# Linear attention and a gated feed-forward in one kernel: batch 0's attention by head halves, another release order of the loads, and a new table of times

## The chip, the cores and the metric

The kernel runs on one core of one Trainium2 chip. The metric is the device time of one execution in microseconds; the time before is the median of three runs. One further execution of each kernel is recorded by the hardware profiler, and all lines of profile shown here come from such records. In them PE is TensorE, DVE VectorE, ACT ScalarE, POOL GpSimd and SP SyncE; L346 is line 346 of the kernel's file.

## What is computed

```python
# q, k, v: (8 batches, 8 heads, 576 tokens, 64) float32;  w_in (512, 2048), w_out (2048, 512) float32
theta = pi/2 * arange(576) / 576
def phi(x):
    r = maximum(x, 0)
    return concatenate([r * cos(theta)[:, None], r * sin(theta)[:, None]], axis=-1)   # 128 features
kv  = einsum('bhsf,bhsd->bhfd', phi(k), v)
z   = sum over the tokens of phi(k)
num = einsum('bhsf,bhfd->bhsd', phi(q), kv)
den = einsum('bhsf,bhf->bhs', phi(q), z)[..., None] + 1e-6
x   = (num / den).transpose(0, 2, 1, 3).reshape(4608, 512)
h   = x @ w_in
out = (h * cos(h)) @ w_out                                                             # (4608, 512) float32
```

## The kernel before

Matrices are held in float16 and accumulated in float32. A batch has 576 tokens: four full tiles of 128 tokens and a remainder of 64. The four full tiles make one chunk of 512 tokens for the feed-forward; the remainders of all eight batches together make a ninth chunk. Chunks 0 to 7 thus follow the batches.

*Attention of one batch.* `load` (L318, L321) brings q, k and v on SP's DMA queue. `prep` (L346 on ACT, L347 on DVE) applies relu and the cosine and sine weights and writes float16 features into the tile `KQ`, one instruction per token tile, and per cosine or sine. `cast_v` (L360 ACT, L361 DVE, L362 POOL) writes v into `V1` beside a column of ones, so that one product gives kv and z. `kv` (L373) runs 40 matmuls (8 heads by 5 token tiles) and copies the result to `kvz`. The q features have to be transposed: for batches 0 and 1 TensorE does it (`q_pe`, L402, with copies to `qT` at L406 and L408); for later batches a DMA transpose on SP's queue does (`q_dma`, L412), which reads `KQ` and writes `qT`. There is one `KQ`, so the next batch's q prep has to wait for those transposes. `num` (L435) multiplies, and three DVE instructions (L451, L453, L455) divide by den; the result is transposed by TensorE (`x_pe`, L475, copy L479) or by a DMA (`x_dma`, L485) into `xT`.

*Feed-forward of one chunk.* `layer1` (L529, chunks 0 and 1; `layer1_plain`, L561, and `layer1_fast`, L667, later) multiplies `xT` by `w_in` into one of four PSUM banks for one group of two 128-column blocks by half of the tokens; `gate` takes the cosine as a Sin on ACT (L502) and multiplies on DVE or POOL (L504). `layer1_fast` and `layer2` (L861) trade matmuls for additions in the manner of Strassen, with copies on ACT (L675, L872) and additions on DVE (L679, L883). `layer2_plain` (L786) is the ordinary second product, used early. Results go through three `ost` buffers to DRAM by DMAs on POOL's queue, some of them accumulating in DRAM.

*What sets the order.* Every piece of work is one step, added to a `Plan` with its reads and writes. Two lists written into the file, `STARTS` (a stamp for each step in hundredths of a microsecond) and `ENGS` (one letter of an engine for each step), fix the engine of each step and the order in which all are issued. The stamps are not waited for on the chip: an engine runs its own steps in the order of their stamps, and waits are semaphores for the data. The 1363 steps of before have stamps from 0 to 275.35 us.

*The head.* `first_attention` (L988) starts with 28 matmuls on unused data (`warm`, L945), loads q whole, k whole and v in two halves of the heads, and takes batch 0 through whole-tile steps; 26 more warm matmuls are spread over the gaps. `weights` (L948) holds the four quarters of `w_in` back by a tiny write on POOL (L950) that reads a piece of k, then issues the four loads on POOL's queue, where they are also turned from float32 to float16 (quarter order 0, 1, 3, 2 by the stamps). A second hold (L960) lets two quarters of `w_out` go after `w_in`'s quarter 0 is there. `second_attention` (L1015) holds batch 1's loads by tiny writes on POOL (`hold_raw`, L975) that read a value of `w_in`'s quarter 2, and `part_of_w_out` (L982) holds the other two quarters of `w_out` until batch 1's q is there (`HOLDW = 1` in the order k, q, v).

```python
def hold():
    nc.gpsimd.tensor_copy(
        out=w_in_sb[0:2, 0, :].rearrange("p (g f) -> p g f", g=4)[:, :, 0],
        in_=raw[ORDER0[1]][0:2, 0, 0, 0:1].broadcast_to((2, 4)))
pl.add("POOL", 0.4, 0.5, 0, hold, hk(ORDER0[1], [0], [0]), [("w_in", g) for g in range(4)])
```

Of the kernel before, what the change touches and what calls it, by code (L numbers as in the profile page):

```python
# [16 lines left out]

STARTS = (
# [166 lines left out]
def kernel(  # L185
# [12 lines left out]
    P = 128  # L198
# [816 lines left out]
    def second_attention():  # L1015
        T = start[1] - 30
        for nm in ORDER1:
# [4 lines left out]
            if nm == ORDER1[HOLDW]:  # L1022
                part_of_w_out(nm, 1)
# [103 lines left out]
```

## Time and profile before

| | before |
|---|---|
| runs, us | 282.57, 281.77, 281.73 |
| median, us | 281.77 |
| profiled execution: span, us | 279.7 |
| PE busy, us | 272.6 (97%), of it warm matmuls 14.7 |
| DVE, ACT, POOL busy, us | 236.9, 210.2, 82.9 |
| mean granted TensorE clock | 1.000 |
| batch 0 landed: q, k, first and second half of v, us | 7.12, 10.43, 12.09, 13.66 |
| `w_in` quarters landed, us | 17.20, 19.72, 22.98, 25.52 |
| `w_out` quarters landed, us | 28.08, 30.79, 44.08, 48.70 |
| batch 1 landed: k, q, v, us | 34.55, 37.86, 40.93 |
| first `layer1` matmul of chunk 1, us | 50.43 |

The span runs from the first to the last instruction of the profiled execution; the time of a run holds some 2 us more. "Landed" is the end of a transfer's last packet, in us from the span's start. A busy PE is one whose matmuls are in flight one behind the other, warm ones included. Releasers behind an arrow name what ended an idle time.

### The profile page before, as it was taken

The numbers are of one execution on the slowest core, as the hardware profiler recorded it, in microseconds if no ns is written. First come the engines' busy times: TensorE is split into PE (matmuls) and PEld (weight loads), VectorE is DVE, ScalarE is ACT, GpSimd is POOL, SyncE is SP. The second block draws the span as 40 slices with busy tenths as digits, with TensorE's granted clock in tenths as the row PEclk, the third lists the DMA queues.
The fourth block names the chain that finished last, engine by engine and source line by source line (L and its number), as shares of the span: only waits on it lengthen the run. The fifth ranks groups of instructions, "written<-read, shape, count | busy, mean of one in ns | idle before, by whom it ended". The sixth has DMA issues, their size and how long they took to land.

```text
span 279.7 us, 6825 instructions
## 1 busy us (share of the span) xinstructions
PE 272.6 (97%) x2698; PEld 215.5 (77%) x2698; DVE 236.9 (85%) x442; ACT 210.2 (75%) x363; POOL 82.9 (30%) x102
## 2 busy tenths in 40 slices
PE   8999999999999999999999999999999999999993
PEld 2567857787966677769777878789988888888882
DVE  1767698989999999999999998989989879873952
ACT  2756699879998897788989988995758686776330
POOL 1430020030501201520340045132534372399210
PEclk9999999999999999999999999999999999999999
DMA  6999989999999999989999998549756495698125
GB/s 207 312 202 206 340 239 241 361 301 174 335 261 271 258 249 246 234 268 259 255 258 246 242 229 284 98 115 141 163 75 139 110 156 105 152 143 123 75 77 150
DMA packets 80223, 58.03 MB, mean 207 GB/s; under 512 B 43200, under 2 KB 77248, under 8 KB 80192
## 3 DMA queue, kind: packets, MB, share of 16 engines
q1 hardware_dynamic: 68960, 39.99, 59.4%
q0 software_dynamic: 10496, 17.04, 30.1%
q10 hardware_dynamic: 736, 0.57, 0.7%
q8 instruction: 21, 0.34, 0.5%
q14 instruction: 10, 0.08, 0.1%
HBM read 36.75 MB, written 11.80 MB: 174 GB/s over the span
## 4 chain that ended last, share of the span: by engine, by line
PE 92%; ACT 3%; DVE 2%; issue 1%; POOL 0%; ACTq 0%; POOLq 0%
PE M L861 34%; PE M L667 14%; PE M L561 11%; PE M L529 9%; PE TR L667 6%; PE ATT L945 5%; PE ATT L435 3%; PE M L786 3%; PE ATT L373 3%; PE TR L561 2%; ACT KQ L346 2%; DVE x L455 1%; PE M L402 1%; PE M L373 0%; PE TR L475 0%
## 5 line engine op out<-in xcount | busy, mean ns | idle before, releaser
L861 PEld LDWEIGHTS <-gT 128*128 128x128 f16 x560 | 53.9, 98 | 8.3
L861 PE MATMUL M<-w_out_sb,gT 128*128 128x256 f16 x448 | 57.1, 273 | 0.0
L504 DVE TENSOR_TENSOR gT<-M,ch 128x512 f16<-128x512 f32 x73 | 48.5, 685 | 5.9 <-ACT ch L502 5.7
L502 ACT ACTIVATE ch<-M 128x512 f32<-128x512 f32 x75 | 43.4, 596 | 12.0 <-PE M L529 5.4
L346 ACT ACTIVATE KQ<-km,CS 128x512 f16<-128x512 f32 x57 | 38.5, 717 | 1.4 <-DMA km<-in_k_dram 1.3
L872 ACT ACTIVATE ost<-M 128x512 f32<-128x512 f32 x41 | 24.3, 596 | 17.9 <-PE M L861 13.0
L346 ACT ACTIVATE KQ<-qm,CS 128x512 f16<-128x512 f32 x46 | 31.5, 720 | 4.1 <-DMA qm<-in_q_dram 4.1
L561 PE MATMUL M<-xT,w_in_sb 128*128 128x512 f16 x136 | 33.8, 379 | 0.0
L861 PE MATMUL M<-T,S 128*128 128x256 f16 x256 | 32.4, 273 | 0.0
L667 PEld LDWEIGHTS <-w_in_sb 128*128 128x128 f16 x288 | 27.3, 98 | 4.8 <-issue 0.3
L362 POOL CAST V<-vm 128x1024 f16<-128x1024 f32 (+1 forms) x18 | 15.9, 907 | 50.8 <-DVE den L451 20.7
L529 PE MATMUL M<-xT,w_in_sb 128*128 128x256 f16 x256 | 30.3, 273 | 0.3 <-DVE gT L504 0.3
L861 PEld LDWEIGHTS <-S 128*128 128x128 f16 x256 | 24.8, 98 | 4.1 <-DVE S L837 0.2
L529 PEld LDWEIGHTS <-w_in_sb 128*128 128x128 f16 x256 | 24.4, 98 | 3.9 <-issue 0.5
L679 DVE TENSOR_TENSOR Z<-M,Z 128x512 f32<-128x512 f32 x31 | 21.1, 687 | 4.3 <-PE M L667 3.1
L561 PEld LDWEIGHTS <-w_in_sb 128*128 128x128 f16 x160 | 14.9, 98 | 12.2
L504 POOL TENSOR_TENSOR gT<-Z,ch 128x512 f16<-128x512 f32 x5 | 6.3, 1268 | 56.6 <-ACT ch L502 20.0
L455 DVE TENSOR_TENSOR x<-ATT,rec 128x512 f16<-128x512 f32 x32 | 22.1, 691 | 1.1
L435 PEld LDWEIGHTS <-qT 128*128 128x128 f16 (+1 forms) x320 | 14.8, 101 | 5.6 <-issue 3.5
L690 ACT ACTIVATE ch<-Z 128x1024 f32<-128x1024 f32 x12 | 12.7, 1057 | 6.9 <-DVE Z L679 4.8
L675 ACT ACTIVATE Z<-M 128x512 f32<-128x512 f32 x26 | 15.1, 596 | 3.4 <-PE M L667 2.4
L435 PE MATMUL ATT<-kvz,qT 128*128 128x65 f16 (+1 forms) x288 | 16.0, 195 | 0.8 <-DVE x L455 0.5
(150 smaller groups left out, 519.3 us busy)
## 6 DMA issues: line engine op xcount, KB each, us to landing
out_dram<-ost POOLq DMA_DIRECT2D x38, 256.0 KB, 4.3
qm<-in_q_dram SPq DMA_DIRECT2D x8, 640.0 KB, 6.7
km<-in_k_dram SPq DMA_DIRECT2D x8, 640.0 KB, 7.1
qm<-in_q_dram SPq DMA_DIRECT2D x8, 512.0 KB, 6.0
km<-in_k_dram SPq DMA_DIRECT2D x8, 512.0 KB, 6.0
vm<-in_v_dram SPq DMA_DIRECT2D x6, 640.0 KB, 5.7
vm<-in_v_dram SPq DMA_DIRECT2D x6, 512.0 KB, 4.6
w_in_sb<-in_moe_w_in_dram POOLq DMA_DIRECT2D x4, 512.0 KB, 8.8
```

The lines of the kernel that those rows point to most:

```text
L346: fn = {"ACT": lambda: nc.scalar.activation(out=out_, in_=in_, func=AF.Relu, scale=sc), "DVE": lambda: nc.vector.tensor_scalar(out=out_, i ...
L362: "POOL": lambda: nc.gpsimd.tensor_copy(out=out_, in_=in_)}
L435: nc.tensor.matmul(bank[hb][ps, hh * D1:(hh + 1) * D1], lhsT=x[:, h, :], rhs=z[:, h, :], start=True, stop=True)
L455: nc.vector.tensor_tensor(out=split(x16[n][:, hs, :], k), in0=A[:, :, :, 0:D], in1=split(rec[n][:, hs], k).unsqueeze(3).broadcast_to((P, k ...
L502: act(0.5, due, lambda: nc.scalar.activation(out=ch[c], in_=bank, func=AF.Sin, bias=math.pi / 2.0, scale=1.0), [key], [("ch", c)])
L504: mul(due, 0.61, lambda q: q.tensor_tensor(out=dst, in0=bank if len(dst.shape) == 2 else bank.rearrange("p (j s) -> p j s", j=dst.shape[1] ...
L529: nc.tensor.matmul(M1[m][:, jj * 2 * P:(jj + 1) * 2 * P], lhsT=w_in_sb[:, cc, j * P:(j + 1) * P], rhs=X[:, cc, ts], start=(cc == 0), stop= ...
L561: nc.tensor.matmul(M, lhsT=w_in_sb[:, cc, j * P:(j + 1) * P], rhs=X[:, cc, :], start=(cc == 0), stop=(cc == NCT - 1))
L667: nc.tensor.matmul(bank[0][:, j * TH:(j + 1) * TH], lhsT=a(cc, j), rhs=b[:, cc, :], start=(first and j == 0 and cc == 0), stop=(last and j ...
L679: dve(0.61, due + 0.3, lambda: nc.vector.tensor_tensor(out=dst, in0=bank[0], in1=dst, op=ALU.add), [bank[1], key], [key])
L861: nc.tensor.matmul(bank[0][:, tt * MH:(tt + 1) * MH], lhsT=a[:, j, tt * P:(tt + 1) * P], rhs=b[:, j, :], start=(first and (apart or tt == ...
L872: act(0.5, due, lambda: nc.scalar.activation(out=dst, in_=view(bank), func=AF.Copy), [bank[1]], dk)
```

## The change

Batch 0 is loaded and computed by halves of the heads: first heads 0 to 3 of q, k and v, then heads 4 to 7, in twelve loads instead of eight (each half of a tensor in two pieces, of 256 and of 320 tokens). A new function, `first_attention_halves`, takes each half through preps, transposes, casts, `kv`, `num`, norm and transpose of x with its own steps: 36 half preps instead of 18, 6 casts of v instead of 10 (DVE, ACT or POOL), 8 half norms instead of 4. The warm matmuls become 20, 12 and 12. `layer1` of chunks 0 and 1 goes through quarters 0 and 1 of `w_in` for the first half of the tokens, then for the second, then through quarters 2 and 3 in the same way.

The loads are let go otherwise: `w_in` waits for the second half of k; its quarters go in the order 0, 1, 2, 3; batch 1's loads wait for quarter 3, which is again the last one; the second half of `w_out` waits for batch 1's v in place of its q. Batch 1's preps may be on either of two engines, its casts of v are 6 instead of 10.

`STARTS` and `ENGS` are replaced wholly: 1409 steps, stamps from 0.74 to 273.04 us. That changes the order of all steps, of the later batches too, though the steps of batches 2 to 7 and of chunks 2 to 8 are the same as before. The rest of the diff (the options `F16`, `MODE`, `SQ`, `H1`, `NUZ`) adds branches that these settings leave unused.

```diff
+OPT = dict(F16=0, FAST1={3: 2, 4: 2, 5: 2, 6: 4, 7: 4, 8: 4}, MODE={}, HH='qkv', LD=[['q', 0], ['k', 0], ['v',
+           0], ['q', 1], ['k', 1], ['v', 1]], NB=[['A0', 'A1'], ['A0', 'A1', 'M0']], XB=[['B3'], ['B3',
+           'M1']], W0=5, W1=6, WF=[[2, 2, 2, 2], [2, 2, 0, 0]], HOLD=['k', 4], RAW1=3, WO2=2, H1=0, W2=0,
+           SQ=0, NUZ=1)
...
-            for quarter in range(4):
-                for hf in range(2):
+            for quarter, hf in ([(q_ + i, hf) for q_ in (0, 2) for hf in range(2) for i in range(2)] if OPT["HH"] else
+                                [(q_, hf) for q_ in range(4) for hf in range(2)]):
...
-                in_=raw[ORDER0[1]][0:2, 0, 0, 0:1].broadcast_to((2, 4)))
+                in_=raw[hn][0:2, hh, 0, 0:1].broadcast_to((2, 4)))
...
+    def copy_by_either(out_, in_, due, dc, ac, rd, wr):
+        both(due, {"DVE": dc, "ACT": ac}, {
+            "DVE": lambda: nc.vector.tensor_copy(out=out_, in_=in_),
+            "ACT": lambda: nc.scalar.activation(out=out_, in_=in_, func=AF.Copy)}, rd, wr)
...
+    def kv_half(hb, bank, key, due, b=0):
...
+            for hh, h in enumerate(hs):
+                for t in range(NT + 1):
+                    nc.tensor.matmul(
+                        bank[:, hh * D1:(hh + 1) * D1], lhsT=kp[:, t, h].rearrange("p g d -> p (g d)"),
+                        rhs=V1[:, t, h, :], start=(t == 0), stop=(t == NT))
...
+    def num_half(t, hb, bank, key, due, b=0):
...
+        dve(0.76, due, norm, [key], [("x16h", n, hb)])
...
+    def half_tiles(hb, due):
...
+        for nm in OPT["HH"]:
+            if nm == "k":
+                for t in range(NT + 1):
+                    for g in range(2):
+                        prep(0, "k", t, g, "", due, hs)
+            elif nm == "v":
+                for t, nt in ((0, 2), (2, 2), (4, 1)):
+                    cast_v(0, t, ("DVE", "ACT", "POOL"), due, hs, nt=nt)
+                kv_half(hb, *BANKS2[hb], due)
+            else:
+                for t in range(NT):
+                    for g in range(2):
+                        prep(0, "q", t, g, "", due, hs)
+                    q_half(t, hb, *BANKS[t], due)
...
+        for t in range(NT):
+            num_half(t, hb, *pick[nb[t % len(nb)]], due + t)
+            n = OPT["WF"][hb][t]
+            if n:
+                warm(n, 0.2157 * n, M1[1], [pick[nb[t % len(nb)]][1]], [("M1", 1)])
+            x_half(t, hb, *pick[kb_[t % len(kb_)]], due + t)
+
+    def first_attention_halves():
...
+        for i in range(OPT["W0"]):
+            warm(4, 1.293)
+        for nm, x in OPT["LD"]:
+            load(0, nm, 0, HALVES if x == 2 else (HALVES[x],))
+        weights()
+        for hb in range(2):
+            half_tiles(hb, 4 + 4 * hb)
...
+            if OPT["HH"]:
+                for t, nt in ((0, 2), (2, 2), (4, 1)):
+                    cast_v(1, t, ("DVE", "ACT", "POOL"), T + 4 + hb, HALVES[hb], nt=nt)
+                continue
...
-    first_attention()
+    (first_attention_halves if OPT["HH"] else first_attention)()
```

More of the change, by code (lines that the diff above doesn't have):

```diff
@@ L282 @@
     ORDER0, ORDER1, HOLDW, W_FIRST = "qkv", "kqv", 1, None
-    GATE1 = (w_in_sb[0:2, 0, Dff // 2 + 1:Dff // 2 + 2], [("w_in", 2)])
+    R1 = OPT["RAW1"]
+    GATE1 = ((w_in_sb[0:2, 0, R1 * Dff // 4 + 1:R1 * Dff // 4 + 2], [("w_in", R1)]) if R1 < 4 else
+             (w_out_sb[0:2, (R1 - 4) * NJT // 4, 1:2], [("w_out", R1 - 4)]))
+    HOLDW = OPT["WO2"]
     src = {"k": k, "v": v, "q": q}
@@ L344, in prep @@
         f = len(heads) / H
-        cost = {"DVE": 0.09 + 0.33 * f, "ACT": 0.12 + 0.5 * f}
+        cost = {"DVE": 0.09 + FD * f, "ACT": 0.12 + 0.5 * f}
         fn = {"ACT": lambda: nc.scalar.activation(out=out_, in_=in_, func=AF.Relu, scale=sc),
@@ L362, in cast_v @@
               "POOL": lambda: nc.gpsimd.tensor_copy(out=out_, in_=in_)}
-        either(due, {e: cost[e] for e in ([eng] if eng else VCAST)}, fn, rd, wr)
+        either(due, {e: cost[e] for e in ([eng] if isinstance(eng, str) else eng)}, fn, rd, wr)
+    full = {}
     def kv(b, due, pair=None):
@@ L398, in q_pe @@
         ps = bank.bitcast(F16).rearrange("p (h s) -> p h s", h=H)
+        more = [("qTh", t % NT, hb) for hb in range(2)] if b == 1 and OPT["HH"] else []
         def mm():
@@ L458, in norm @@
                     op=ALU.mult)
-        dve(1.05 if pair is None else 1.15, due, norm, keys, [("x16", n)])
+        dve(1.05 if pair is None else 1.15, due, norm, keys, [("x16", n)]
+            + ([("x16h", n, hb) for hb in range(2)] if b == 1 and OPT["HH"] else []))
         return n
@@ L577 @@
     LATE = min(c for c, nf in FAST1.items() if nf > 2)
-    assert all(FAST1[c] == NJT // 4 for c in range(LATE, NC))
     def flat(t, dt=F16):
@@ L754, in store @@
             five, four = rows(c)
[L755 to L756 removed]
+            Q = (nc.sync, "SP") if OPT["SQ"] else (nc.gpsimd, "POOL")
+            put(due, five[:, 2 * h:2 * h + 2, :], blocks(O, n), keys, *Q)
+            put(due, four[:, 2 * h:2 * h + 2, :], blocks(O, 1 - n), keys, *Q)
             return
@@ L951, in hold @@
                 out=w_in_sb[0:2, 0, :].rearrange("p (g f) -> p g f", g=4)[:, :, 0],
-                in_=raw[ORDER0[1]][0:2, 0, 0, 0:1].broadcast_to((2, 4)))
-        pl.add("POOL", 0.4, 0.5, 0, hold, hk(ORDER0[1], [0], [0]), [("w_in", g) for g in range(4)])
+                in_=raw[hn][0:2, hh, 0, 0:1].broadcast_to((2, 4)))
+        hn, hh = OPT["HOLD"] if OPT["HH"] else (ORDER0[1], 0)
+        pl.add("POOL", 0.4, 0.5, 0, hold, hk(hn, [hh], [0]), [("w_in", g) for g in range(4)])
         for g in range(4):
@@ L1013, in first_attention, with both @@
             x_pe(0, t, t, *BANKS[3 - t % 2], "ACT", 8 + t, [("fill", t)])
+    def both(due, cost, fn, rd, wr, lat={"DVE": 0.13, "ACT": 0.15}):
+        pl.add([(e, cost[e], cost[e] + lat[e], fn[e]) for e in cost], 0, 0, due, None, rd, wr)
+    def copy_by_either(out_, in_, due, dc, ac, rd, wr):
+        both(due, {"DVE": dc, "ACT": ac}, {
+            "DVE": lambda: nc.vector.tensor_copy(out=out_, in_=in_),
+            "ACT": lambda: nc.scalar.activation(out=out_, in_=in_, func=AF.Copy)}, rd, wr)
@@ new lines, in q_half, with mm @@
+    def q_half(t, hb, bank, key, due):
+        hs = HALVES[hb]
+        ps = bank.bitcast(F16)[:, 0:HB * P].rearrange("p (h s) -> p h s", h=HB)
+        full[key] = False
+        def mm():
+            for hh in range(HB):
+                nc.tensor.matmul(ps[:, hh, :], lhsT=qp[:, t, hb * HB + hh].rearrange("p g d -> p (g d)"),
+                                 rhs=IDENT, is_transpose=True)
+        pe(HB, MMT, due, mm, [("qp", t, g, h) for g in range(2) for h in range(H)[hs]] + ["ID"], [key])
+        copy_by_either(qT[t][:, hs, :], ps, due, 0.4, 0.5, [key], [("qTh", t, hb)])
@@ new lines, in num_half, with mm, norm @@
+    def num_half(t, hb, bank, key, due, b=0):
+        n = t if b == 0 else xcount[0] % NX
+        full[key] = False
+        hs = HALVES[hb]
+        def mm():
+            for hh in range(HB):
+                nc.tensor.matmul(bank[:, hh * D1:(hh + 1) * D1], lhsT=qT[t][:, hb * HB + hh, :],
+                                 rhs=kvz[b][:, hb * HB + hh, :], start=True, stop=True)
+        pe(HB, MMA, due, mm, [("qTh", t, hb) if b == 0 else ("qT", t), ("kvz", b, hb)], [key])
+        A = bank[:, 0:HB * D1].rearrange("p (h d) -> p h d", h=HB)
+        def norm():
+            nc.vector.tensor_scalar_add(out=den[n][:, hs], in0=A[:, :, D], scalar1=1e-6)
+            nc.vector.reciprocal(out=rec[n][:, hs], in_=den[n][:, hs])
+            nc.vector.tensor_tensor(out=x16[n][:, hs, :], in0=A[:, :, 0:D],
+                                    in1=rec[n][:, hs].unsqueeze(2).broadcast_to((P, HB, D)), op=ALU.mult)
+        dve(0.76, due, norm, [key], [("x16h", n, hb)])
@@ new lines, in x_half, with mm @@
+    def x_half(t, hb, bank, key, due, after=(), b=0, n=None):
+        n = t if b == 0 else n
+        full[key] = False
+        cs = slice(hb * NCT // 2, (hb + 1) * NCT // 2)
+        ps = bank.bitcast(F16)[:, 0:NCT // 2 * P].rearrange("p (c s) -> p c s", c=NCT // 2)
+        x2 = x16[n].rearrange("p h d -> p (h d)")
+        def mm():
+            for i, c in enumerate(range(NCT)[cs]):
+                nc.tensor.matmul(ps[:, i, :], lhsT=x2[:, c * P:(c + 1) * P], rhs=IDENT, is_transpose=True)
+        pe(NCT // 2, MMT, due, mm, [("x16h", n, hb), "ID", *after], [key])
+        copy_by_either(xT[b][:, cs, t * P:(t + 1) * P], ps, due, 0.28, 0.36, [key] + ([("xTh", b, t)] if hb else []),
+                       [("xT", b, t) if hb else ("xTh", b, t)])
@@ L1025, in second_attention @@
             for g in range(2):
-                prep(1, "k", t, g, "DVE" if g == 0 else "ACT", T + 1)
+                prep(1, "k", t, g, E1 or ("DVE" if g == 0 else "ACT"), T + 1)
         for t in range(NT + 1):
@@ L1029, in second_attention @@
             for g in range(2):
-                prep(1, "q", t, g, "DVE" if g == 0 else "ACT", due)
+                prep(1, "q", t, g, E1 or ("DVE" if g == 0 else "ACT"), due)
             if t < NT:
@@ L1033, in second_attention @@
         for hb in range(2):
+            if OPT["HH"]:
+                for t, nt in ((0, 2), (2, 2), (4, 1)):
+                    cast_v(1, t, ("DVE", "ACT", "POOL"), T + 4 + hb, HALVES[hb], nt=nt)
+                continue
             for t in range(NT + 1):
                 cast_v(1, t, "ACT" if t % 2 else "DVE", T + 4 + hb, HALVES[hb])
+        if OPT["H1"]:
+            for hb in range(2):
+                kv_half(hb, ATT[:, hb, :], ("ATT", hb), T + 6, 1)
+            for hb in range(2):
+                for t in range(NT):
+                    num_half(t, hb, ATT[:, t % 2, :], ("ATT", t % 2), T + 8 + t, 1)
+                    x_half(t, hb, *(BANKS[3], BANKS[2])[t % 2], T + 8 + t, (), 1, xcount[0] % NX)
+                    xcount[0] += 1
+            q_pe(1, NT, *BANKS[3], "ACT", start[1] + 10)
+            n = num(1, NT, start[1] + 12)
+            x_pe(1, NT, n, *BANKS[3], "ACT", start[1] + 12)
+            return
         kv(1, T + 6)
@@ L1051, in attention @@
         for t, nt in ((0, 2), (2, 2), (4, 1)):
-            cast_v(b, t, "POOL", T + 6 + 0.4 * t, nt=nt)
+            cast_v(b, t, ("POOL", "DVE") if OPT["F16"] else "POOL", T + 6 + 0.4 * t, nt=nt)
         kv(b, T + 8)
```

165 lines of the change are left out of this document (117 added, 48 removed), and 198 rows, old and new, of the table STARTS.

## Prediction

> **What bounds the kernel now.** I began with the page: busy times, slices, chain.
>
> ```profile
> span 279.7 us, 6825 instructions
> PE 272.6 (97%) x2698; PEld 215.5 (77%) x2698; DVE 236.9 (85%) x442; ACT 210.2 (75%) x363; POOL 82.9 (30%) x102
> DMA  6999989999999999989999998549756495698125
> PE 92%; ACT 3%; DVE 2%; issue 1%; POOL 0%; ACTq 0%; POOLq 0%
> ```
>
> TensorE is busy 272.6 of 279.7 us and carries 92% of the chain. So only two things can move the end: time in which TensorE has no useful matmul, and new waits in a run that has none. 2.1 us lie around the span (281.77 - 279.7). The profiled execution thus agrees with the median of the three runs, and I add differences to 281.77. About 0.3% (0.85 us) is what a measurement of this kernel can tell from no change.
>
> Next the timeline of the first 35 us, PE and POOL rows, for the time without useful matmuls.
>
> ```profile
> 1.32 9.04 PE L945 MATMUL ATT<-S 128*128 128x512 f16 x28 [1.32 <-POOL S L931]
> 10.57 0.19 POOL L950 CAST w_in_sb<-km 2x4 f16<-2x4 f32 x1 [9.09 <-DMA km<-in_k_dram]
> 11.13 3.46 POOL L956 DMA_DIRECT2D w_in_sb<-in_moe_w_in_dram  x4 [0.37 <-POOL w_in_sb L950]
> 17.25 0.20 POOL L960 COPY w_out_sb<-w_in_sb 1x4 f16<-1x4 f16 x1 [2.67 <-DMA w_in_sb<-in_moe_w_in_dram]
> 23.88 10.71 PE L529 MATMUL M<-xT,w_in_sb 128*128 128x256 f16 x96 [0.27 <-DVE gT L504]
> 25.67 0.18 POOL L975 CAST km<-w_in_sb 2x1 f32<-2x1 f16 x1 [6.44 <-ACT ch L502]
> ```
>
> L945 is filler. The dense run of `layer1` begins at 23.88 us; two of its groups (8 matmuls each) run before, at 21.20 and 22.36. POOL's holds (L950, L960, L975) show when loads are let go.
>
> Then the windows table, to see what cover there is later.
>
> ```profile
> 100.00:125.00 25.00, 25.00 (x256) 19.51 (x256) 23.88 (x47) 20.14 (x35) 7.30 (x9) 1.00 1.05 248
> 150.00:175.00 25.00, 25.00 (x263) 19.54 (x262) 23.92 (x45) 21.82 (x38) 7.12 (x10) 1.00 1.09 242
> 175.00:200.00 25.00, 25.00 (x265) 21.05 (x263) 23.10 (x42) 19.33 (x35) 6.68 (x7) 1.00 0.74 121
> ```
>
> Columns: window and length, then PE, PEld, DVE, ACT, POOL busy, clock, DMA share, GB/s. Up to 175 us TensorE is full, the DMA engines are full too (share over 1), DVE has 1.1 us of slack in 25 and ACT 3 to 5. A late transfer has little to hide behind.
>
> Last the rows of L412, the transposes of q by DMA.
>
> ```profile
> L412 SPq DMA_TRANSPOSE qT<-KQ x27: 1241/1832/3132, 59.8 to 195.1; - x27
> DMA to landing us min/median/max: 3.0/5.2/8.2
> ```
>
> SP holds its queue 1.83 us (median) for one of them, and it lands 5.2 us after its issue.
>
> **Part 1, the head.** Both orders move the same 3.54 MB of batch 0, one load after the other, so the last piece of v still lands near 13.66 us. What shrinks is the work behind it. Now: casts until about 14.8, `kv` 15.21 to 16.58, copy, `num`, norm, transposes, first group at 21.20. After: a half cast on POOL or ACT to about 14.9; 20 kv matmuls, 0.62 (half of the 40 that take 1.37, less the overlap); kvz copy 0.4; four `num` matmuls 0.13; a half norm 0.76 (the plan's figure; whole norms are planned at 1.05 to 1.15); x transposes 0.2; their copy 0.4; with some 0.15 of hand-over at each of seven steps, about 18.6. Bounds from the rows: 18.0, if hand-overs overlap, to 20.0, if each half costs as much as a whole.
>
> The weights move the other way. The hold of `w_in` waits for the fifth of six half pieces. These are the bytes of q, k and v's first half now; the cast of that half began at 12.37, k was in at 10.43, and the hold ran at 10.57. So the hold comes about 1.57 later. The quarters now land at 17.20, 19.72, 22.98 and 25.52; after, at about 18.8, 21.3, 24.5 and 27.1. In the new order the first two groups need quarter 0 (18.8), the third needs quarter 1: the dense run starts at 21.3, not 23.88. Gain 2.6 us; 1.6 if the half chain is at its slow end, 3.3 if the weights run faster in an emptier queue. Ten fillers fewer (44, not 54) cost nothing: they stand where TensorE waits for data, and the clock column is 1.00 from the first filler on. The 36 half preps and 8 half norms cost more per element than 18 and 4 whole ones, but lie under loads until 13.66.
>
> **Part 2, what the head hands on.** `w_out`'s first half follows quarter 0, batch 1's loads follow the weights, 1.57 later. Batch 1's v lands at 40.93 now, about 42.5 after. The second half of `w_out` (38.49, released by q at 37.86; landed 44.08 and 48.70) is held for v: about 2.6 later, 46.7 and 51.3. TensorE's work before `layer1` of batch 1 (50.43) is whatever `layer2_plain` has weights for; one group (1.73 us, 8 matmuls) falls behind it, and TensorE stands idle some 2 to 2.5 us between 40 and 50. The 2.6 is given back: at 50 us I take 0, between -1 (one group more fits in) and +1.
>
> How the DMA queues share decides the size of this. From 26 to 29 us five loads were issued on SP's queue while POOL's was full:
>
> ```profile
> q0 software_dynamic: 608, 0.60, 122.0%
> q1 hardware_dynamic: 14, 0.01, 1.4%
> ```
>
> SP's loads (q1) moved almost nothing until POOL's (q0) were through, so batch 1's loads start late by the whole delay of the weights. [...]
>
> **Part 3, the new table, 50 to 200 us.** Every engine runs its steps in the table's order, and the stamps of before are close to its trace: after 50 us each TensorE step began within -1.3 to +0.1 us of its stamp, each ACT and DVE step within -1.5 to +1.1. So the distance, in the table, from a transfer's issue to the first step that needs it is the room it has.
>
> Before: q transposes had room of 7.5 us (median; least 5.9) against 5.2 measured; 640 KB loads 9.3 (least 6.7) against 5.8 (4.9 to 9.6). After: q transposes 5.1 (least 2.8), and 14 of 27 have less than the measured median; 640 KB loads 7.0 (least 4.8), 4 of 15 short. The bytes are the same and DMA is full, so I see no reason for them to land sooner. The step that then waits is mostly the next batch's q prep (L346) on ACT, which overwrites the transpose's source; behind it in ACT's order stand the Sin of the gates (L502) and the copies (L872, L675) that free TensorE's banks. Of these a few stand free, each 0.87 us of matmuls; between 96 and 112 us, as an example, ACT's longest idle piece in the trace of before is 1.19 us, so a wait of over 2 us goes through to TensorE.
>
> I count one shortage per batch, the largest, since a stall shifts all later stamps of that batch alike (issue -> use in the table, room, 5.22 less room): 66.58 -> 70.29, 3.71, 1.51; 84.82 -> 89.37, 4.55, 0.67; 103.18 -> 105.98, 2.80, 2.42; 129.85 -> 133.25, 3.40, 1.82; 146.90 -> 149.80, 2.90, 2.32. Sum 8.7 us. If all land in the shortest 3.05: 0.25 + 0.15, say 0.4, or nothing behind slack. With the longest 8.2, 4.5 + 3.7 + 5.4 + 4.8 + 5.3 = 24. I take the median: the trace of before has queues just as full.
>
> **Part 4, the tail.** After 200 us POOL's stores of 256 KB leave their buffers at rooms of 2.5 to 3.2 us in the table, against 2.4 to 4.3 measured (median 3.1). Three such places at up to 0.6, and the accumulating stores (room 6.9, measured 6.8 to 8.7) at 0.3: +1.0; between 0 and +3.
>
> Sum: 281.77 + 0 + 8.7 + 1.0 = 291.5 us.
>
> **The rivals.** *The room suffices: faster.* The table's last stamp falls 2.3 us (275.35 to 273.04). If q transposes land at a median of 3.5 us or less, most of the five places above close and the head's gain stays: 281.77 - 2.3 = 279.5. For it: the shortest was 3.05, and fewer transfers are ahead where spacing differs. Against: 5.2 at a DMA share over 1, with unchanged bytes. It decides at 281.77 - 0.85: shortages in sum under 1.4 us.
>
> *A backlog: much slower.* The new table sets SP's steps behind a transpose 1.25 us apart (98.00, 99.25, 100.50), where the trace has 1.83. Six in a batch give 3.5 us late at the last, on top of the shortage at two or three batches: 8.7 + 1 + 3 x 3.5 = +20, less what single shortages already count; 300.
>
> *Mostly absorbed.* ACT's 3 to 5 us of slack per 25, and the banks, swallow about 1 us at each place: 0.51 + 0 + 1.42 + 0.82 + 1.32 = 4.1 is left, and the tail's stores hide: 281.77 + 4.1 = 285.9.
>
> *No net change.* The head's gain of 2.6 stays and stalls cost as much: 281.8.
>
> **How the numbers follow.** Forecast 0.57 (its own range 287 to 297: three places of five, or all with 1 us more); backlog 0.15; absorbed 0.12; faster 0.13; none 0.03. The range leaves out the faster case and the far part of the backlog: 281 to 302. Faster 0.13, same 0.03, slower 0.84.
>
> **What the profile after would show.** Head: dense `layer1` from about 21.3 us, `w_in`'s hold at about 12.1; wrong if later than 22.5. By 50 us: TensorE idle 2 us or more, `layer1` of batch 1 near 50. Middle: TensorE idle in pieces of 1 to 3 us in the windows 50 to 175, ACT's idle before L346 released by a DMA, L412 still at 5 us. The forecast is wrong if those windows stay full, or if the idle is ended by DVE with no transfer behind it.

## The result and the profile after

The changed kernel took 301.79 us (median of 4 runs, 301.44 to 302.56) against 282.11 for the kernel before in the same comparison: a ratio of 1.0705, 95% interval 1.0684 to 1.0725, 19.7 us slower. The prediction said 291.5 us, so the direction was right and the size half of what came.

The same lines of the page, after:

```profile
span 299.8 us, 6858 instructions
PE 277.3 (92%) x2688; PEld 215.8 (72%) x2688; DVE 237.9 (79%) x456; ACT 209.7 (70%) x365; POOL 97.9 (33%) x112
DMA  6899999999999999989999576324676376767115
PE 47%; DMA 17%; DVE 11%; issue 10%; POOL 7%; ACT 6%; SPq 2%; DVEq 0%; POOLq 0%; ACTq 0%
```

The span grew by 20.1 us, PE's busy time by 4.7. The chain tells more: before, TensorE carried 92% of it and transfers none; now TensorE has 47% and DMA 17%. The transfers in the chain, in order of time (start, length, what):

```profile
78.24 10.02 DMA vm<-in_v_dram
...
92.57 8.08 DMA qT<-KQ
...
151.39 7.37 DMA qm<-in_q_dram
...
186.80 5.73 DMA xT<-x
...
206.44 3.40 DMA out_dram<-ost
...
242.09 6.62 DMA gT<-S
```

A load of v, a q transpose, a load of q, an x transpose, a store and an accumulating transfer: all kinds, over the whole span.

The head, PE and POOL:

```profile
1.32 7.23 PE L1014 MATMUL ATT<-S 128*128 128x512 f16 x20 [1.32 <-POOL S L1000]
13.34 0.19 POOL L1019 CAST w_in_sb<-km 2x4 f16<-2x4 f32 x1 [2.05 <-DMA km<-in_k_dram]
18.12 0.77 PE L1112 MATMUL M<-V,KQ 128*128 128x65 f16 x20
22.44 2.17 PE L553 MATMUL M<-xT,w_in_sb 128*128 128x256 f16 x16
24.67 12.54 PE L553 MATMUL M<-xT,w_in_sb 128*128 128x256 f16 x112
```

The hold of `w_in` ran at 13.34 (10.57 before), the second half's `kv` at 18.12, and the dense run of `layer1` began at 24.67, where it had begun at 23.88.

The windows, PE first, then PEld, DVE, ACT and POOL:

```profile
100.00:125.00 25.00, 21.99 (x229) 16.11 (x227) 21.75 (x44) 17.89 (x31) 4.71 (x7) 1.00 1.06 258
150.00:175.00 25.00, 23.76 (x253) 18.61 (x252) 20.65 (x41) 20.56 (x36) 8.59 (x6) 1.00 0.77 166
175.00:200.00 25.00, 23.10 (x222) 17.66 (x220) 21.53 (x36) 16.77 (x30) 5.12 (x8) 1.00 0.55 127
```

Windows in which TensorE had been full have 1.2 to 3.0 us of idle now, and DVE and ACT are idle with it: all three wait.

The q transposes (now L432), and the two DMA queues from 29 to 32 us, when batch 1's loads stood behind the weights:

```profile
L432 SPq DMA_TRANSPOSE qT<-KQ x27: 1232/1628/4371, 62.8 to 212.3; - x27
DMA to landing us min/median/max: 3.0/4.9/9.7
```

```profile
q0 software_dynamic: 583, 0.57, 116.4%
q1 hardware_dynamic: 54, 0.06, 5.5%
```

A transpose takes about what it took (median 4.9 against 5.2; between 55 and 175 us 5.96 against 5.65). It is the room in front of its user that shrank (by the tables 7.5 us in the median before, 5.1 after). From 29 to 32 us SP's loads again moved little beside POOL's (54 packets to 583): SP's first packet came 2.9 us after the first issue of these loads (28.73), at 31.62. In the kernel before, it took 4.0 us for the loads issued from 42.20 on, behind `w_out`; at the start of both kernels, with nothing on POOL's queue, 1.5. The prediction's 608 packets to 14, from 26 to 29 us, overstate it somewhat, since by the 1.5 us at the start I estimate that about half of the 2.9 us before SP's first packet there (issued 25.88, first packet 28.77) would have passed without POOL's as well. Nor is it so everywhere: from 51.0 to 52.5 us in the changed kernel POOL's queue moved 182 packets and SP's 176.

To say where the time went I count *useful work behind*: the TensorE work (warm matmuls left out, each step at its length at full clock) that is still to do at a moment, less the same for the kernel before. The total, 255.7 us, is the same in all kernels here; the grain is one group, 0.9 us, so smaller differences in the table mean little.

| us behind at | 25 | 50 | 60 | 100 | 150 | 175 | 225 | 270 |
|---|---|---|---|---|---|---|---|---|
| changed kernel | 0.8 | 2.1 | 4.6 | 7.9 | 13.1 | 14.0 | 17.5 | 19.6 |
| head_only | 0.8 | 2.2 | 9.0 | 8.8 | 9.6 | 8.6 | 9.2 | 8.7 |
| head_only_60 | 0.8 | 2.2 | 4.6 | 6.0 | 6.3 | 6.6 | 7.0 | 6.9 |
| table_only | 0.0 | 2.0 | 6.3 | 8.8 | 14.8 | 16.9 | 19.2 | 21.8 |
| old_tail | 1.9 | 2.5 | 3.5 | 7.9 | 12.5 | 12.5 | 14.4 | 14.8 |
| after_light | 1.8 | 2.5 | 3.5 | 3.6 | 5.9 | 5.9 | 9.2 | 11.3 |
| half_transposes | 0.8 | 2.2 | 4.6 | 5.3 | 8.2 | 9.6 | 13.1 | 15.2 |
| tail_light | 0.8 | 2.1 | 2.9 | 7.1 | 11.7 | 13.0 | 14.4 | 14.8 |
| old_release | 0.0 | 2.9 | 8.6 | 11.8 | 18.5 | 19.3 | 21.5 | 23.9 |
| before_light | 0.0 | -0.2 | 0.0 | 0.0 | 0.0 | 0.0 | 0.0 | 0.0 |

The changed kernel lost 4.6 us up to 60 us, 9.4 from there to 175, and 5.6 after. At 200 us, where the prediction has the tail begin, it was some 16 us behind.

### The profile page after: what moved, and what is told of

Same layout as the page of the kernel before. It is cut to its first block, busy times and chain, and to the rows that moved or that the text cites. A ratio compares the mean times of both kernels' runs of the same rounds, so it can differ in the third digit from the quotient of the medians.

```text
span 299.8 us, 6858 instructions
## 1 busy us (share of the span) xinstructions
PE 277.3 (92%) x2688; PEld 215.8 (72%) x2688; DVE 237.9 (79%) x456; ACT 209.7 (70%) x365; POOL 97.9 (33%) x112
## 4 chain that ended last, share of the span: by engine, by line
PE 47%; DMA 17%; DVE 11%; issue 10%; POOL 7%; ACT 6%; SPq 2%; DVEq 0%; POOLq 0%; ACTq 0%
PE M L930 16%; PE M L553 7%; PE M L714 6%; PE M L586 5%; DMA qm<-in_q_dram 4%; PE M L855 3%; DMA vm<-in_v_dram 3%; DMA xT<-x 3%; DMA qT<-KQ 3%; ACT KQ L361 2%; PE TR L714 2%; DMA gT<-S 2%; DVE gT L527 2%; ACT ch L525 2%; POOL gT L743 2%
## 5 line engine op out<-in xcount | busy, mean ns | idle before, releaser
L361 ACT ACTIVATE KQ<-qm,CS 128x512 f16<-128x512 f32 (+1 forms) x53 | 34.1, 685 | 13.2 <-DMA qT<-KQ 8.0
L377 POOL CAST V<-vm 128x1024 f16<-128x1024 f32 (+2 forms) x22 | 17.9, 845 | 63.5 <-PE M L553 12.5
L361 ACT ACTIVATE KQ<-km,CS 128x512 f16<-128x512 f32 (+1 forms) x55 | 35.0, 679 | 1.4 <-DMA km<-in_k_dram 1.4
L714 PEld LDWEIGHTS <-w_in_sb 128*128 128x128 f16 x288 | 27.6, 97 | 7.7 <-issue 2.4
L553 PE MATMUL M<-xT,w_in_sb 128*128 128x256 f16 x256 | 32.5, 280 | 0.5 <-DVE gT L527 0.3
L553 PEld LDWEIGHTS <-w_in_sb 128*128 128x128 f16 x256 | 25.1, 100 | 4.9 <-issue 1.2
L586 PEld LDWEIGHTS <-w_in_sb 128*128 128x128 f16 x160 | 14.9, 97 | 15.2 <-issue 3.6
L799 POOL DMA_DIRECT2D out_dram<-ost x20 | 11.2, 563 | 34.9 <-DVE ost L952 18.0
L476 DVE TENSOR_TENSOR x<-ATT,rec 128x512 f16<-128x512 f32 x30 | 20.7, 691 | 1.0
L812 POOL DMA_DIRECT2D out_dram<-ost x12 | 13.8, 1256 | 20.7 <-ACT ost L941 14.4
L743 POOL TENSOR_TENSOR gT<-Z,ch 128x1024 f16<-128x1024 f32 x6 | 14.5, 2418 | 14.7 <-ACT ch L737 10.5
L455 PEld LDWEIGHTS <-qT 128*128 128x128 f16 (+1 forms) x288 | 13.5, 101 | 7.7 <-issue 3.0
L455 PE MATMUL ATT<-kvz,qT 128*128 128x65 f16 (+1 forms) x272 | 14.5, 194 | 3.7 <-DMA qT<-KQ 1.6
```

Source lines behind the costliest of these rows:

```text
L361: fn = {"ACT": lambda: nc.scalar.activation(out=out_, in_=in_, func=AF.Relu, scale=sc), "DVE": lambda: nc.vector.tensor_scalar(out=out_, i ...
L455: nc.tensor.matmul(bank[hb][ps, hh * D1:(hh + 1) * D1], lhsT=x[:, h, :], rhs=z[:, h, :], start=True, stop=True)
L476: nc.vector.tensor_tensor(out=split(x16[n][:, hs, :], k), in0=A[:, :, :, 0:D], in1=split(rec[n][:, hs], k).unsqueeze(3).broadcast_to((P, k ...
L553: nc.tensor.matmul(M1[m][:, jj * 2 * P:(jj + 1) * 2 * P], lhsT=w_in_sb[:, cc, j * P:(j + 1) * P], rhs=X[:, cc, ts], start=(cc == 0), stop= ...
L586: nc.tensor.matmul(M, lhsT=w_in_sb[:, cc, j * P:(j + 1) * P], rhs=X[:, cc, :], start=(cc == 0), stop=(cc == NCT - 1))
L714: nc.tensor.matmul(bank[0][:, j * TH:(j + 1) * TH], lhsT=a(cc, j), rhs=b[:, cc, :], start=(first and j == 0 and cc == 0), stop=(last and j ...
```

## The experiments

### Head and table apart

**head_only**: the new head, the old order from 50 us on.

```diff
 # after.py
-STARTS, ENGS: new for all 1409 steps
+steps that before has at 50 us or later: before's stamps and engines; the others: the new ones
```

> The changed kernel's steps with its own order up to a stamp of 50 us, and the order and engines of before for every step that before has at 50 us or later. Theory 1 (the new table leaves transfers too little room after 50 us, and the head is a smaller, separate loss): the useful TensorE work of the changed kernel was 4.8 us behind at 55 us, and with the old order nothing is added after that: 282.1 + 4.8 = 287, between 285 and 289. Rival (the later weights and loads of the head upset all that follows, whatever the table): 296 or more. Second rival (the halves of batch 0 cost nothing and all 20 us are the table's): 282 to 283.

Measured: 290.77 us (ratio 1.0303, 1.0266 to 1.0341), 8.5 slower. From 60 us to the end nothing was added (9.0 to 8.7 behind), as theory 1 has it; but 4.4 us more than expected were lost at the seam, where the old order calls for a group of `layer2_plain` whose `w_out` was not there.

**head_only_60**: the same with the seam at 60 us.

```diff
-steps that before has at 50 us or later
+steps that before has at 60 us or later
```

> As the kernel with the new head alone, but the old order takes over at a stamp of 60 us instead of 50. In that run TensorE stood idle for 5.0 us at 50.2 and 1.7 at 55.3, because the old order asks for a group of layer2_plain with the second half of w_out before the first layer1 of batch 1, and that half landed only at 55.26 (the new release waits for v). Theory 1: here that group comes later, the kernel is 4.6 us behind at 60 us like the changed kernel, and nothing is added: 282.2 + 4.6 = 286.8, between 285 and 288.5. Rival (the head itself costs 8.5 us, wherever the orders meet): 290 to 291.

Measured: 287.06 us (1.0166, 1.0132 to 1.02), 5.0 slower. 4.6 us behind at 60 us, 6.9 at the end; the 2.3 between were not taken apart. The head's price is thus close to 5 us, some 1.5 of it a fall of the clock (0.50 from 52 to 54 us; part 2 below), and the table makes the rest, by its order and its engines, which were not told apart: with the same steps, the windows are full again.

```profile
75.00:100.00 25.00, 25.00 (x263) 18.88 (x260) 24.24 (x47) 23.06 (x43) 6.72 (x9) 1.00 1.11 283
100.00:125.00 25.00, 25.00 (x253) 18.37 (x251) 23.82 (x45) 19.90 (x35) 5.42 (x8) 1.00 1.15 250
```

**table_only**: the old head, the new order from 50 us on.

```diff
 # before.py
-STARTS, ENGS: those of before
+steps that the new table has at 50 us or later: the new stamps and engines; the others: before's
```

> The kernel before with its own order up to 50 us, and the order and engines of the changed kernel for every step that the new table has at 50 us or later. Theory 1: the changed kernel lost 19.6 - 4.8 = 14.8 us of useful TensorE work between 55 us and the end, and does so here: 282.1 + 14.8 = 297, between 294 and 300. Rival (the head upsets what follows): 282 to 286. If head and table add up, this excess and that of the kernel with the new head alone sum to 19.7.

Measured: 304.47 us (1.0788, 1.075 to 1.0826), 22.2 slower: more than the changed kernel. The seam costs 6.3 us by 60 us here, so the sum of the two excesses, 30.7, is not 19.7 as additivity would have it. From 60 us on, though, 15.5 us were lost (6.3 to 21.8), against 15.0 in the changed kernel (4.6 to 19.6) with another head. Both windows below belong to this kernel:

```profile
75.00:100.00 25.00, 22.97 (x239) 16.83 (x236) 20.30 (x40) 21.10 (x38) 3.73 (x5) 1.00 1.18 284
100.00:125.00 25.00, 22.24 (x232) 16.29 (x230) 20.93 (x41) 16.75 (x30) 3.73 (x6) 1.00 1.03 240
```

### Is it the transfers?

**after_light** and **before_light**: the loads of batches 2 to 7 with half of their bytes, in the changed kernel and in the one before.

```diff
 def load(b, nm, due, hs=(slice(0, H),)):
     for h in hs:
+        if b > 1:
+            h = HALVES[0]
         five, four = tokens(src[nm][b][h])
```

> The changed kernel, but q, k and v of batches 2 to 7 are loaded for heads 0 to 3 only: half the bytes of these loads are left out, with all else as it was. Theory 1: q transposes and loads land sooner (about 4 us for a transpose instead of 5.7), and most of the 9.3 us lost between 55 and 175 us come back; the head and the tail stay: 301.8 - 8 = 294, between 292 and 296. Rival (TensorE waits for what ACT and DVE do in the new order, not for transfers): 300 to 302.

> The kernel before, with q, k and v of batches 2 to 7 loaded for heads 0 to 3 only (half the bytes of these loads left out). Theory 1: in the old order transfers have room enough, so sooner landings free nothing: 282.2, between 281.3 and 282.6, where the same cut took 7.8 us off the changed kernel. Rival (TensorE pays for DMA traffic in either order, at its ports or otherwise): 275 to 280.

Measured: 294.04 us (1.042, 1.0376 to 1.0463), 7.8 less than the changed kernel, and 281.93 us (0.9995, 0.9981 to 1.001), no change. In both, a q transpose now lands in about 4 us:

```profile
L434 SPq DMA_TRANSPOSE qT<-KQ x27: 1232/1300/2186, 61.8 to 203.6; - x27
...
  ACT KQ L363: 2.6, 4
...
DMA to landing us min/median/max: 3.1/4.0/6.0
```

(This is the changed kernel with light loads; "ACT KQ L363: 2.6, 4" are the us and times that q preps waited for it. In the changed kernel they were 8.0 and 5.) Between 60 and 175 us 2.4 us were lost in place of 9.4. The kernel was also only 3.5 us behind at 60 us, not 4.6: this profiled run lacks the changed kernel's fall of the clock at 51 us (its clock is 1.00 from 46 to 60; part 2 below). The old order gains nothing from the same relief: it had room to spare, and TensorE paid nothing there for the other half of these loads (281.93 us against 282.10).

**half_transposes**: whole loads, q transposes with half of their bytes.

```diff
-            out=dst, in_=qp[:, t].rearrange("p h g d -> p (h g d)"), transpose=True),
+            out=dst[:, 0:nh], in_=qp[:, t, 0:nh].rearrange("p h g d -> p (h g d)"), transpose=True),
```

with `nh = HB if t < NT else H`.

> The changed kernel, but each q transpose by DMA moves heads 0 to 3 only (half its bytes left out); all loads are whole. Halving the loads took 7.8 us off and brought the median of a q transpose between 55 and 175 us from 5.96 to 3.98 us. Theory 1a (a transpose is late because it stands behind loads): its own half saves at most some 0.8 us for each place, 2 to 4 us in all: 298 to 300. Theory 1b (it is late by its own length): as much as with light loads, 292 to 296. Rival (transfers do not matter): 301 to 302.

Measured: 297.41 us (1.0567, 1.053 to 1.06). The saving is 4.4 us, a little above the 2 to 4 of theory 1a and short of the light loads. A transpose's time to landing hardly changed (median 4.8 us against 4.9; 4.0 with light loads), which speaks for 1a: it is late for what stands ahead of it more than for its own length. That is not shown cleanly, since SP's hold of its queue for one fell as well (median 1.63 to 1.26 us), and what stands behind it may have gone sooner for that.

**old_release**: the weights and `w_out` let go earlier.

```diff
-           'M1']], W0=5, W1=6, WF=[[2, 2, 2, 2], [2, 2, 0, 0]], HOLD=['k', 4], RAW1=3, WO2=2, H1=0, W2=0,
+           'M1']], W0=5, W1=6, WF=[[2, 2, 2, 2], [2, 2, 0, 0]], HOLD=['q', 4], RAW1=2, WO2=1, H1=0, W2=0,
```

> The changed kernel with earlier releases: w_in waits for the second half of q (11.58 us) instead of k (13.21), batch 1's loads for quarter 2 of w_in instead of 3, and the second half of w_out for batch 1's q (40.4) instead of its v (43.5); the order of all else is kept. Theory 1: w_in lands about 1.6 us and w_out's second half 3 to 4 us sooner; 1 to 2.5 us of the 4.6 lost before 60 us come back, nothing later: 301.8 - 1.7 = 300, between 298.5 and 301. Rival (the release order is behind most of the 20 us): under 295. Rival (the attention of batch 0 and 1 sets these times, not the weights): 301.5 to 302.

Measured: 305.93, 306.53 and 309.03 us in three runs, 311.01 in a fourth; without that one 306.53 in the median (1.0898, 1.0842 to 1.0954), some 5 us worse, where all three theories had it equal or better. The second half of `w_out` did leave earlier (issued 39.39 in place of 43.21), but now ahead of batch 2's k, which landed at 51.75 and 53.24 in place of 45.69 and 47.09. What that does is seen in two lines of ACT and one of PE:

```profile
51.84 0.72 ACT L349 ACTIVATE KQ<-km,CS 128x512 f16<-128x512 f32 x1 [5.68 <-DMA km<-in_k_dram]
52.47 1.00 ACT L414 ACTIVATE qT<-M 128x1024 f16<-128x1024 f16 x1
```

```profile
53.52 0.58 PE L485 MATMUL M<-IDENT,x 128*128 128x128 f16 x4 [6.60 <-ACT qT L414]
```

A k prep for batch 2, which nobody needs yet, stands first in ACT's order and waits 5.68 us for its load; behind it stands the copy of qT for batch 1, and TensorE is idle for 6.60 us. PE's releaser is ACT, the cause a transfer. The clock, too, is at a half from 51.1 to 57.9 us (0.77, 0.50, 0.50 and 0.76 in the windows 50 to 52, 52 to 54, 54 to 56 and 56 to 60).

### The head

**half_loads**: the kernel before with batch 0's loads in halves.

```diff
-            load(0, nm, 0, HALVES if nm == ORDER0[2] else (slice(0, H),))
+            load(0, nm, 0, HALVES)
```

> The kernel before with q, k and v of batch 0 each loaded in two halves of the heads (twelve loads instead of eight), in the order q, k, v; nothing else changed. Theory 1: loads of half the heads are slower, as in the changed kernel, where the same 3.54 MB were in at 14.72 us instead of 13.66; here the last piece lands at about 14.7 and the time is 282.2 + 0.5 to 1.1. Rival (they are slower in the changed kernel because of what else it does in that time): 13.7 us, and 282.

Measured: the last piece landed at 15.06 us (13.66 before, 14.72 in the changed kernel); the time was 282.19 us (1.0011, 0.9995 to 1.0027), which cannot be told from no change. So the halves are in later here too, with the old head's work beside them, but 1.4 us there cost this head at most 0.8 (0.0027 of 282). From 5 to 10 us the DMA's busy share and rate in the changed kernel (first fence) and before (second):

```profile
5.00:10.00 5.00, 5.00 (x32) 2.58 (x31) 3.54 (x13) 3.44 (x9) 0.00 (x0) 1.00 0.89 278
```

```profile
5.00:10.00 5.00, 5.00 (x20) 2.05 (x19) 2.07 (x5) 1.95 (x3) 0.00 (x0) 1.00 1.08 362
```

In half_loads they were 0.98 and 327, between the two, though its last piece landed latest: the rate of these 5 us is not the halves' doing alone.

**head_kv_first**: `kv` of the second half four steps earlier in TensorE's queue.

```diff
 # head_only_60, TensorE's order
-num(t=3, half 0), warm, q_half, x_half, kv(half 1)
+kv(half 1), num(t=3, half 0), warm, q_half, x_half
```

> The kernel with the new head up to 60 us and the old order after it (287.1); one step is moved in TensorE's queue: kv of the second half of the heads, whose casts were done at 16.7 us and which began at 18.1, goes ahead of the first half's third num, which waits for a bank until 17.2. Theory 2 (the second half's chain is late because it stands in order behind the first half's): the dense run of layer1 starts 0.6 to 1.3 us sooner than 24.7, and the time is 286.1, between 285.5 and 286.6. Rival (DVE's eight norms of 0.83 us in series set that start, wherever kv stands): 287.1, no change.

Measured: `kv` began at 16.81 in place of head_only_60's 18.30, and the dense run at 24.58 in place of 24.86: theory 2 fell, and the start hardly moved, as the rival had it. That the norms alone set it is not shown: in the chain of this run two norms stand behind `kv`, with two copies on DVE between them, and then a `num`, two fillers and transposes of q. The time, 285.48 us (1.0117, 1.008 to 1.0155), is 1.6 below head_only_60 for another reason: in that kernel's profiled run the clock fell at 51 us (mean 0.994), in this one it did not between 50 and 60. A run of head_only_60 in which it did not (mean clock 1.000) took 285.5.

**head_no_fill**: without the 24 fillers among the half steps.

```diff
-           'M1']], W0=5, W1=6, WF=[[2, 2, 2, 2], [2, 2, 0, 0]], ...
+           'M1']], W0=5, W1=0, WF=[[0, 0, 0, 0], [0, 0, 0, 0]], ...
```

> The kernel with the new head up to 60 us and the old order after it (287.1), without the 24 warm matmuls that are spread through batch 0's half steps (the first 20 stay). The forecast held that fillers cost nothing. Theory 2 (they stand in TensorE's queue ahead of useful steps: x_half was ready at 13.87 in the changed kernel and started at 14.78, behind four fillers that waited for the same bank): the dense run of layer1 starts about 1 us sooner than 24.7, and 286. Rival (they keep the granted clock up; without them it falls to a half while TensorE waits for data, and the first 3 to 4 us of the dense run go at half speed): 288.5 or more.

Measured: 293.6 us (1.0419, 1.0389 to 1.0449), 6.5 above head_only_60. The rival was right:

```profile
14.00:18.00 4.00, 2.47 (x33) 0.50 0.73 101
...
24.00:26.00 2.00, 2.00 (x11) 0.50 1.23 206
26.00:28.00 2.00, 2.00 (x22) 1.00 1.20 186
```

(PE alone: busy us and matmuls, granted clock, DMA share, GB/s.) The clock is at a half from 14 to 26 us, and again at 54 to 62. In the changed kernel, with the same head and these fillers, it is 1.00 from 10 to 30 us: the fillers do not wait beside the useful steps for nothing.

### The tail

**old_tail**: the changed kernel with the old order from 165 us on.

```diff
-STARTS, ENGS: new for all steps
+steps that before has at 165 us or later: before's stamps and engines
```

> The changed kernel with the order and engines of before for every step that before has at 165 us or later. Theory 1: the changed kernel was 14.0 us behind at 175 us and 19.6 near the end; the 5.6 between come from short rooms of x transposes, stores and accumulating stores in the new order, and go with the old one: 301.8 - 5.6 = 296.2, between 295 and 298. Rival (the tail is late because POOL and DVE have more work there, not because of its order): 300 to 302.

Measured: 297.45 us (1.055, 1.0492 to 1.0608), 4.3 less. From 175 us on 2.3 us were lost in place of 5.6; the rest is from before, most of it the clock's fall at 51 us, which this profiled run does not have (clock 1.00 from 46 to 60 us; 3.5 behind at 60, not 4.6).

**tail_light**: the changed kernel with half of the bytes in the stores of chunks 4 to 7 and in the accumulating transfers.

```diff
 def put(...):
+        if nb == 256.0 and LIGHT[0]:
+            dst, src_ = dst[:, :, 0:MH], src_[:, :, 0:MH]
...
 def accum(dst, src_, kb, rd, wr, due):
+        dst, src_ = dst[0:P // 2], src_[0:P // 2]
```

> The changed kernel, but the stores to DRAM of chunks 4 to 7 and the accumulating transfers of layer2 move half of their bytes only (the other half is left out). The changed kernel lost 14.0 us up to 175 us and 5.6 more behind it; there stores landed in 3.3 to 4.2 us against rooms of 2.5 to 3.0, and accumulating ones in 6.6 and 9.4 against 6.9 and 9.3. Theory 1 (the tail waits for these transfers and for x transposes): 2 to 3.5 of the 5.6 us come back: 301.8 - 2.8 = 299, between 298 and 300. Rival (the tail waits for POOL and DVE themselves): 301.3 or more.

Measured: 298.06 us (1.0574, 1.0524 to 1.0625), 3.7 less. The profiled run took 296.91, 4.9 less: 1.8 us were lost after 175 us (13.0 to 14.8) in place of 5.6, and 2.9 up to 60 us in place of 4.6, since the clock did not fall at 51 us (mean 1.000); the middle lost 0.7 more. The tail, too, waits for transfers.

### One that told nothing

**reordered**: the changed kernel's steps on the same engines, in an order from a search of my own.

```diff
-STARTS: the new table
+STARTS: an order found by moving single steps within an engine's queue, judged by planned durations and a first-in-first-out model of the transfers
```

> The changed kernel with the same steps on the same engines, but another order within each engine's queue, from a search that moved steps so that what waits for a transfer stands later and work that can go stands ahead of it. Theory 1 (the order gave transfers too little room): most of the 15 us lost after 60 us come back; the head stays, whose kernel with the old order took 287.1: 287 to 291. Rival (the choice of engines or the split steps themselves cost the 20 us, not the order): 297 or more.

Measured: 330.9 us (1.1766, 1.1712 to 1.1821). It was 11.3 us behind at 45 us already, since the search had moved the head's steps as well, and 47 at the end. It does not test theory 1, and what made it slow was not taken apart; the mean granted clock was 0.958.

## Why the prediction was right and wrong

By its own borders, 50 and 200 us, the prediction added up 0 + 8.7 + 1.0; the runs show 2.1, some 14 and some 3.5 us. The steps that failed are the head, where a gain of 2.6 us was to pay for the idle behind it and there was no gain, and the waits for transfers: it priced five q transposes and the tail's stores, and put loads, x transposes and the clock at nothing.

**Part 1, the head: wrong.** "The dense run starts at 21.3 us, not 23.88. Gain 2.6 us": it began at 24.67, with two groups right ahead of it from 22.44; by useful work the kernel was 0.8 us behind at 25. Three terms of the sum were mis-sized. The loads: "the last piece of v still lands near 13.66"; it landed at 14.72, and the fifth of six pieces at 13.21, so the hold ran at 13.34, not 12.1, and the quarters landed at 19.43 and 22.03 (18.8 and 21.3 forecast). The cast: done at 16.7, not 14.9, since POOL's part stood behind two issues of weights (13.89 to 15.58) that waited for the hold, and ACT's behind preps of k. And the chain of one half: I counted one norm of 0.76; the first group needs two tiles, whose second norm ends at 21.73 after a first at 20.52 (0.83 each, with a `num` between them that waits for the bank). The second tile's copy was done at 22.03; two fillers and transposes of q, whose copy on ACT ended at 22.15, still stood ahead of the group. head_kv_first shows that the place of `kv` is not what set the start; how it divides between norms, copies and fillers stays open. "Ten fillers fewer cost nothing" holds for 54 to 44 (clock 1.00 up to 50 us); it does not hold for 44 to 20, 6.5 us.

**Part 2, what the head hands on: the idle came, the sum was wrong.** I forecast 2.0 to 2.5 us of idle between 40 and 50, "given back" from a gain that was not there; TensorE was idle for 1.3 us there (0.2 before), and waited for batch 1's copy of qT and its norms. From 25 to 60 us 3.8 us were lost. The second half of `w_out` landed at 50.57 and 54.91, not 46.7 and 51.3. About 1.5 us more come from something that the prediction did not have, the granted clock:

```profile
48.00:49.00 1.00, 0.54 (x9) 1.00 1.25 201
49.00:50.00 1.00, 0.51 (x14) 1.00 1.15 199
50.00:51.00 1.00, 0.77 (x15) 1.00 1.13 225
51.00:52.00 1.00, 1.00 (x8) 0.63 1.17 245
52.00:53.00 1.00, 1.00 (x9) 0.50 1.15 261
...
54.00:55.00 1.00, 1.00 (x11) 0.66 1.07 381
```

In the changed kernel TensorE was idle in pieces between 47.6 and 51 us, and from about 51.3 to 54.7, for 3.4 us, its clock was at a half: two groups of `layer1` took 1.54 and 1.68 in place of 0.87, 1.5 us together. The longest single idle piece ahead of that was 0.81 us, in three us that were 0.5 to 0.8 busy; what made the clock fall there is not shown.

**Part 3, the table: right in mechanism, too small, and wrong in most places.** Forecast 8.7 us between 50 and 200; some 14 came: 2.5 from 50 to 60, 1.5 of them the clock, 9.4 from 60 to 175, and some 2 from there to 200, with a late x transpose. That 8.7 is near the 9.4 of the middle is in good part luck, as the places show. The step "no reason for them to land sooner" held (5.96 us against 5.65). Where the waits fell is another matter. These are the transfers behind which the engines' delay against the table grew (issue in the trace; us to landing; room in the table; us that were added):

| transfer | issued | took | room | added |
|---|---|---|---|---|
| q transpose | 73.94 | 7.86 | 6.08 | 1.1 |
| v load | 78.24 | 10.02 | 6.74 | 0.7 |
| q transpose | 89.23 | 5.75 | 4.62 | 1.6 |
| q transpose | 92.57 | 8.08 | 4.55 | 2.1 |
| q transpose | 111.70 | 6.39 | 3.94 | 2.0 |
| q transpose | 121.72 | 7.51 | 4.26 | 1.4 |
| q load | 151.39 | 7.37 | 5.55 | 2.0 |
| x transpose | 186.80 | 5.73 | 4.00 | 1.9 |
| store | 206.44 | 3.40 | 2.69 | 1.1 |
| store | 230.68 | 4.17 | 2.98 | 1.5 |

Of the five places that I named only one is here (stamp 84.82, issued at 92.57), and it cost 2.1, not 0.67. The smallest rooms (2.80 at 103.18, 2.90 at 146.90) made no wait: a stall just ahead in ACT's queue had moved their users back and given them time. That each batch stalls once or twice was right; the choice of the smallest room was not. The v load's row has another path: the kernel's text orders its steps marked `port` on DVE and POOL one behind the other, so that DVE had to wait for POOL's cast of that load.

```profile
88.38 2.05 POOL L377 CAST V<-vm 128x1024 f16<-128x1024 f32 x2 [2.16 <-DMA vm<-in_v_dram]
90.46 1.23 DVE L906 TENSOR_TENSOR S<-gT 128x2048 f16<-128x2048 f16 x1 [0.63 <-POOL V L377]
```

In one of the q transposes' places ACT and PE look like this:

```profile
100.68 0.72 ACT L361 ACTIVATE KQ<-qm,CS 128x512 f16<-128x512 f32 x1 [1.59 <-DMA qT<-KQ]
101.31 0.58 ACT L941 ACTIVATE ost<-M 128x512 f32<-128x512 f32 x1
```

```profile
101.94 1.03 PE L930 MATMUL M<-T,S 128*128 128x256 f16 x8 [1.68 <-ACT ost L941]
```

The q prep waits 1.59 us for the transpose of the features that it overwrites, the copy that frees TensorE's bank stands behind it, and TensorE waits 1.68: the chain that the prediction described, a wait of under 2 us included, which it had thought the banks could cover.

**Part 4, the tail: right kind, wrong size.** +1.0 forecast for the time after 200 us, some 3.5 measured (5.6 from 175 on). I priced stores and accumulating transfers by what a late one exceeds its room, 0.3 to 0.6 each, with the median; a store that takes 4.17 at a room of 2.98 exceeds it by 1.2. The x transposes (room 4.00, took 5.73, still in the stretch of part 3) I had not looked at.

**The rivals.** "The room suffices" fell. The backlog's 300 us is the nearest figure, but its mechanism did not show: SP's issue of a transpose had a median of 1.63 us, and in four of the five rows above with a q transpose SP had issued with less delay against the table than the engine that then waited had (92.57: 7.75 us, ACT 9.54; the other way at 89.23 alone, 8.39 to 8.03). The time came near it by luck: the stretches up to 60 and from 175 us on added 10.2 us to the 9.4, and no pile-up of queues showed. "Mostly absorbed" fell: in these places little was.

## What to carry to other kernels

When an order is fixed by hand or by a planner, compare for every transfer the distance from issue to first user with the measured time to landing, its spread too, and not for one kind only: here an order whose q transposes had 7.5 us of room for 5.2 was insensitive to halving the load traffic, and one with 5.1 lost 9.4 us between 60 and 175, but 2.4 with half of it. Price the head of a kernel by the whole chain in the order of each queue (every tile that the first group needs, every issue that stands ahead), and when a change empties TensorE in pieces, ask what the clock does (here it fell to a half for 3.4 us). A planner's gain of 2.3 us on paper is worth nothing unless its durations hold on the chip with their spread.

## What the runs showed of the hardware

In the changed kernel the granted clock fell to a half for 3.41 us, after three us at 0.5 to 0.8 busy, with no idle piece over 0.81 us; it did not fall in every run of a kernel (head_only_60: 285.5 us at a mean clock of 1.000, 287.0 to 288.0 at 0.990 to 0.994). How busy TensorE is does not settle it: from 46 to 50 us it was busy for 2.69 us in the changed kernel, and for 2.59 in table_only and 2.68 in head_kv_first, whose clock stayed at 1.00 from 46 to 60. The slow stretches that the windows up to 66 us show lasted 3.4 us (after, head_only_60), 6.8 (head_only, old_release), and 13.6 and 10.2 (head_no_fill); what sets their start and length is not shown. Loads of 0.26 and 0.33 MB in place of 0.52 and 0.66 landed 1.1 (changed kernel) and 1.4 us (half_loads) later in all, with issues 0.65 us apart in the changed kernel, and moved 278 and 327 GB/s in place of 362 from 5 to 10 us; what limits them was not looked into.
